# First layer over all pieces, then the second layer in blocks of 512 tokens with a seven-product second matmul, on one pool of 4 KB tiles

## The chip, the cores and the metric

The kernel runs on one core of one Trainium2 chip. The metric is the device time of one execution in microseconds (us); the time of the kernel before is the median of its runs. All on-chip work is written in Bass and Tile: the program's text gives each engine's work, a scheduler at build time sets the order in each engine's queue, and a queue is then executed in that order.

## What is computed

A chunked state-space scan (a small recurrent attention) feeds two feed-forward layers. With 4 sequences of 768 tokens there are 3072 tokens of 256 features.

```python
attn_out = _attn_ref(x, a, B, C)               # scan over chunks of 32 tokens, 8 heads of 32
x = attn_out.transpose(0, 2, 1, 3).reshape(3072, 256)
h = x @ w_in1                                  # 256 -> 2048
x = np.maximum(0.01 * h, h) @ w_out1           # 2048 -> 256
h = np.maximum(x @ w_in2, 0.0)                 # 256 -> 2048
out = (h * h) @ w_out2                         # 2048 -> 256
```

The reference computes in double precision where weights are double. The kernel reaches its accuracy by splitting each operand into a high and a low part (both fp32r), so that each product of two operands is three matmuls: high x low, high x high and low x high.

## The kernel before

**Pieces and scans.** The tokens are cut into 12 pieces of 256 tokens (`NP`, `TP`). `scan_piece` computes the scan of one piece in 20 or 22 steps (`QN`; it is a generator, and each `yield` ends a step). Its chain is: scaled copies (`him`, `ch`, L324 and L325, on ScalarE), the low part `kmx` (L331, VectorE), four small DMAs that lay it out block-diagonally (`diag`, L318, issued by SyncE), 32 matmuls `S` (L348, L349), the masked products `mk` (L358, VectorE), `mkh` (L360, ScalarE) and `mkl` (L365, VectorE), 48 matmuls `Y` (L373 to L375), the state (`d1s` L377 on ScalarE, a scan `stt` L213 on VectorE, `shl` L382 and L384, a transpose L386), four more small DMAs of the state (`sbd`, L318), 32 matmuls into `Y` (L393, L394, here called `Z`), and at last `yh` (L397, ScalarE) and `yl` (L398, VectorE), which are the first layer's input. A piece's state goes into the next piece. For each later sequence, `sequence_scales` loads its pieces once more (`all`, L276) and takes sums of squares (`sq`, L235).

**Layers.** `Phase` is one layer over a block of one or two pieces (`BLOCKS`: four of one piece, 256 tokens wide, then four of two, 512 wide). Per step, `hmm` makes the first product for one or two tiles `m` of 128 of the 2048 features (L425 to L427, 6 matmuls for each m), `act` evicts it (layer 1: two activations L435 and L436 and a subtraction L441; layer 2: a ReLU L438, a square L439 on VectorE, a copy L440 and the subtraction L441), and `omm` adds the second product for it into the two PSUM tiles `o` (L453, L454, L458, also 6 matmuls for each m), two or three steps later (`LAG`). `finish` writes layer 1's result back over its input (L466, L467) or stores layer 2's (L471, L472).

**Order.** A table gives the order of the blocks; the first digit is the layer, the second the block:

```python
ORDER = "10 11 12 20 13 21 14 22 23 15 24 16 25 17 26 27"
```

Between the steps of this loop the main program advances the scans (`step_to(due(...))`), so that a block's scan is written ahead of its first layer, spread over the time since the block before.

**Weights.** The four matrices come as doubles, in 8 chunks each of 512 KB. `w_step` moves the pipeline on by one chunk: load (L121), two passes on ScalarE (L130, L133), two on VectorE (L141, L142), then high part (L153, ScalarE) and low part (L154, VectorE). All four matrices are needed by the time of the first layer-2 block.

**Memory.** Weights, inputs and working tiles lie in pools of their own (`cp`, `sp`, `wp`, `yp`); the accumulators `o` have one buffer each (pool `po`), the first product three (`ph`), the scan's `S` and `Y` one each (`pz`).

## Time and profile before

| what | value |
| --- | --- |
| median of 3 runs | 634.33 us (633.23 to 635.82) |
| profiled execution, its own time | 637.78 us |
| its span, first to last instruction | 636.1 us |
| TensorE busy | 586.2 us (92%), 4434 matmuls |
| VectorE busy | 402.6 us (63%) |
| ScalarE busy | 372.9 us (59%) |
| DMA queue | 45.76 MB, 27.8% of 16 engines |

A busy TensorE is not TensorE at its peak: a matmul's record runs on while the next one has begun, so that the distance between two starts tells what one costs, not its length. Shares are averages over stages: in the first 100 us ScalarE and VectorE are busy almost all the time, later TensorE is. The difference between the span and the profiled execution's own time (1.7 us) lies outside the program's instructions.

### The profile page before, as it was taken

How to read it: one execution, taken by the hardware profiler on the slowest of the kernel's cores; microseconds unless marked ns; L12 is line 12 of the kernel's file. 1: busy time of each engine (PE TensorE's matmuls, PEld its weight loads, DVE VectorE, ACT ScalarE, POOL GpSimd, SP SyncE). 2: the span in 40 equal slices, each digit the busy share in tenths (PEclk: the TensorE clock that was granted, in tenths of full speed). 3: DMA queues.
4: the chain of work that ended last, by engine and by line, in shares of the span. 5: the costliest groups of instructions: out<-in, count | busy, mean ns of one | idle time of the engine just before them, and what ended most of it. 6: DMA issues, size and time to landing. Idle time of an engine off the chain costs nothing.

```text
span 636.1 us, 11298 instructions
## 1 busy us (share of the span) xinstructions
PE 586.2 (92%) x4434; PEld 516.9 (81%) x4434; DVE 402.6 (63%) x687; ACT 372.9 (59%) x678; POOL 5.2 (1%) x14
## 2 busy tenths in 40 slices
PE   0297698999989999999999999999999999999997
PEld 0287698989989888899988888888888888888885
DVE  6999999995558664576564576564565322555553
ACT  6999998876555545545545555455544433544442
POOL 3000000000000000000000000000000000000000
PEclk9999898999989999999999999999999999999999
DMA  7886565555351412202212212212000000000000
GB/s 272 275 291 195 139 205 98 174 124 127 105 94 40 74 51 26 50 35 42 51 51 26 49 36 25 51 67 26 9 1 9 34 1 1 0 2 0 34 1 33
DMA packets 111396, 46.47 MB, mean 73 GB/s; under 512 B 94320, under 2 KB 101104, under 8 KB 111344
## 3 DMA queue, kind: packets, MB, share of 16 engines
q1 hardware_dynamic: 111344, 45.76, 27.8%
q8 instruction: 35, 0.57, 0.4%
q14 instruction: 17, 0.14, 0.1%
HBM read 36.83 MB, written 3.15 MB: 63 GB/s over the span
## 4 chain that ended last, share of the span: by engine, by line
PE 76%; ACT 9%; DVE 6%; DMA 6%; issue 2%; SPq 1%; DVEq 0%; ACTq 0%
PE o L453 12%; PE hp L425 12%; PE hp L427 12%; PE hp L426 12%; PE o L458 12%; PE o L454 12%; DMA all<-in 2%; DMA in<-in 2%; ACT wst L130 1%; ACT wst L133 1%; ACT sq L235 1%; SPq L318 1%; ACT t L436 1%; ACT gh L435 1%; DVE e L195 1%
## 5 line engine op out<-in xcount | busy, mean ns | idle before, releaser
L441 DVE TENSOR_TENSOR gl<-t,gh 128x512 fp32r<-128x512 f32 x192 | 132.3, 689 | 139.5 <-ACT t L436 85.9
L435 ACT ACTIVATE gh<-hp 128x512 fp32r<-128x512 f32 x96 | 57.2, 596 | 84.1 <-PE o L454 75.6
L425 PE MATMUL hp<-yl,wh1i 128*128 128x256 f32 (+1 forms) x256 | 89.5, 350 | 10.8 <-DVE yl L398 4.6
L440 ACT CAST gh<-t 128x512 fp32r<-128x512 f32 x96 | 59.5, 620 | 66.3 <-DVE t L439 56.2
L439 DVE TENSOR_TENSOR t<-t 128x512 f32<-128x512 f32 x96 | 66.2, 689 | 43.4 <-ACT t L438 43.1
L438 ACT ACTIVATE t<-hp 128x512 f32<-128x512 f32 x96 | 57.4, 598 | 56.7 <-PE hp L427 54.5
L453 PE MATMUL o<-gh,wl1o 128*128 128x256 f32 (+1 forms) x256 | 84.9, 347 | 4.5 <-DVE wl1o L154 3.6
L426 PE MATMUL hp<-yh,wh1i 128*128 128x256 f32 (+1 forms) x256 | 88.6, 346 | 0.0
L427 PE MATMUL hp<-yh,wl1i 128*128 128x256 f32 (+1 forms) x256 | 88.4, 345 | 0.0
L426 PE MATMUL hp<-yh,wh2i 128*128 128x256 f32 (+1 forms) x256 | 86.0, 336 | 0.0
L425 PE MATMUL hp<-yl,wh2i 128*128 128x256 f32 (+1 forms) x256 | 86.0, 336 | 0.0
L427 PE MATMUL hp<-yh,wl2i 128*128 128x256 f32 (+1 forms) x256 | 86.0, 336 | 0.0
L453 PE MATMUL o<-gh,w2o 128*128 128x256 f32 (+1 forms) x256 | 83.6, 343 | 1.6 <-DVE yl L467 1.5
L454 PE MATMUL o<-gh,wh1o 128*128 128x256 f32 (+1 forms) x256 | 83.0, 340 | 0.0
L454 PE MATMUL o<-gh,w2o 128*128 128x256 f32 (+1 forms) x256 | 81.9, 336 | 0.0
L425 PEld LDWEIGHTS hp<-yl,wh1i 128*128 128x128 f32 x256 | 51.3, 200 | 16.7 <-DVE ss L256 3.8
L458 PE MATMUL o<-gl,wh1o 128*128 128x256 f32 (+1 forms) x256 | 60.5, 339 | 0.0
L458 PE MATMUL o<-gl,w2o 128*128 128x256 f32 (+1 forms) x256 | 60.3, 336 | 0.0
L453 PEld LDWEIGHTS o<-gh,wl1o 128*128 128x128 f32 x256 | 48.9, 191 | 10.6 <-DVE wl1o L154 4.7
L436 ACT ACTIVATE t<-hp 128x512 f32<-128x512 f32 x96 | 57.1, 594 | 0.0
L426 PEld LDWEIGHTS hp<-yh,wh1i 128*128 128x128 f32 x256 | 51.3, 200 | 5.1 <-issue 0.3
L427 PEld LDWEIGHTS hp<-yh,wl1i 128*128 128x128 f32 x256 | 51.0, 199 | 5.1
(123 smaller groups left out, 984.8 us busy)
## 6 DMA issues: line engine op xcount, KB each, us to landing
in<-in SPq DMA_DIRECT2D x12, 640.0 KB, 4.6
in<-in SPq DMA_DIRECT2D x12, 512.0 KB, 3.4
all<-in SPq DMA_DIRECT2D x15, 384.0 KB, 3.7
wst<-w1i SPq DMA_DIRECT2D x8, 512.0 KB, 7.9
wst<-w1o SPq DMA_DIRECT2D x8, 512.0 KB, 5.8
wst<-w2o SPq DMA_DIRECT2D x8, 512.0 KB, 5.1
wst<-w2i SPq DMA_DIRECT2D x8, 512.0 KB, 4.7
out_t<-ob SPq DMA_DIRECT2D x8, 256.0 KB, 2.2
```

The costliest lines, as they stand in the source:

```text
L425: nc.tensor.matmul(hp, wh, self.xl[:, :, k], start=(k == 0), stop=False)
L426: nc.tensor.matmul(hp, wh, self.xh[:, :, k], start=False, stop=False)
L427: nc.tensor.matmul(hp, wl, self.xh[:, :, k], start=False, stop=(k == KI - 1))
L435: nc.scalar.activation(gh, hp, AF.Lrelu)
L436: nc.scalar.activation(t, hp, AF.Lrelu)
L438: nc.scalar.activation(t, hp, AF.Relu)
L439: nc.vector.tensor_tensor(t, t, t, ALU.mult)
L440: nc.scalar.copy(gh, t)
L441: nc.vector.tensor_tensor(gl, t, gh.bitcast(F32), ALU.subtract)
L453: nc.tensor.matmul(self.o[d], wl, gh, start=(m == 0), stop=False)
L454: nc.tensor.matmul(self.o[d], wh, gh, start=False, stop=False)
L458: nc.tensor.matmul(self.o[d], wh, gl, start=False, stop=(m == KO - 1))
```

## The change

All of layer 1 comes first, block after block (`BLOCKS` is now six blocks of one piece and three of two), with the scans `RATE` = 1.5 steps per tile `m` ahead; then all of layer 2, in six groups of 512 tokens. Layer 2's second product is written by Strassen's algorithm: features `j` and `j + 8`, the two halves of the outputs and the two halves of the tokens make a 2 x 2 by 2 x 2 block product, which takes seven block products (of 128 x 128 by 256 tokens) where the plain form has eight. For that, the weights of `w_out2` get four sums (`split_w1`), the squared activations get four sums `ts` (`act` of `Two`), and the seven results are added up at the end of a group (`finish` of `Two`). The square goes from VectorE to ScalarE. The result of layer 1 is kept in fp32 (`yf`) and split by `split_y` for a whole group. Weights, piece inputs and working tiles come from one pool, `heap`, of 46 tiles of 4 KB per partition. Weights of layer 2 are prepared in smaller portions (`w_one`) while layer 1 runs.

```diff
@@ -34,12 +34,17 @@
 E23 = float(1 << 23)
 QN = [22] * NPC + [20] * (NP - NPC)
 
-BLOCKS = [1, 1, 1, 1, 2, 2, 2, 2]
-GROUPS = [[0, 1], [2, 3], [4], [5], [6], [7]]
-
-ORDER = "10 11 12 20 13 21 14 22 23 15 24 16 25 17 26 27"
+BLOCKS = [1, 1, 1, 1, 1, 1, 2, 2, 2]
+NG = NP // 2
 LAG = {1: 2, 2: 3}
+LAG2 = 2
 W_AHEAD = 4
+RATE = 24 / KO
+NHEAP = 46
+
+
+A11, A12, A22, S1, S3, S2, S4 = 1, 3, 2, 4, 5, 6, 7
+T1, T3, T2, T4 = range(4)
...
-    wp = ctx.enter_context(tc.tile_pool(name="wp", bufs=8))
-    yp = ctx.enter_context(tc.tile_pool(name="yp", bufs=2))
+    heap = ctx.enter_context(tc.tile_pool(name="heap", bufs=NHEAP))
...
+
+    def big(shape, dtype, name):
+        return heap.tile(shape, dtype, tag="b", name=name)
...
     def split_w1():
 
-        nm, c, sl, w0, w1 = w_half.pop(0)
+        nm, c, w0, w1 = w_half.pop(0)
         nc.vector.scalar_tensor_tensor(w0, w1, 3, w0, ALU.logical_shift_left, ALU.bitwise_or)
-        nc.vector.scalar_tensor_tensor(w0, w1, -(1 << 31), w0, ALU.bitwise_and, ALU.bitwise_or)
-        w_full.append((nm, c, sl, w0.bitcast(F32)))
+        if nm != "2o":
+            nc.vector.scalar_tensor_tensor(w0, w1, -(1 << 31), w0, ALU.bitwise_and, ALU.bitwise_or)
+            w_full.append((nm, c, w0.bitcast(F32)))
+            return
+        a = big([P, 8, P], F32, "wa")
+        nc.vector.scalar_tensor_tensor(
+            a[:, 0:4].rearrange("p (k d) f -> p k (d f)", k=2).bitcast(I32),
+            w1, -(1 << 31), w0, ALU.bitwise_and, ALU.bitwise_or,
+        )
+        nc.vector.scalar_tensor_tensor(a[:, S1], a[:, 0], -1.0, a[:, A22], ALU.mult, ALU.subtract)
+        nc.vector.tensor_tensor(a[:, S3], a[:, A11], a[:, 0], ALU.subtract)
+        nc.vector.scalar_tensor_tensor(a[:, S2], a[:, S1], -1.0, a[:, A11], ALU.mult, ALU.subtract)
+        nc.vector.tensor_tensor(a[:, S4], a[:, A12], a[:, S2], ALU.subtract)
+        w_full.append((nm, c, a[:, 1:8]))
 
     def split_w2():
 
-        nm, c, sl, w = w_full.pop(0)
+        nm, c, w = w_full.pop(0)
         if nm == "2o":
-            t = w_last[c] = wp.tile([P, 2, 2, 256], F32R, tag="w", name="w2o")
+            h, l = w_done[nm, c] = tuple(big([P, 7, P], F32R, x) for x in ("wh", "wl"))
+        else:
+            t = w_done[nm, c] = big([P, 2, 2, 256], F32R, f"w{nm}")
             h, l = t[:, 0], t[:, 1]
-        else:
-            h, l = w_hi[nm][sl], w_lo[nm][sl]
         nc.scalar.activation(h, w, AF.Copy)
         nc.vector.tensor_tensor(l, w, h.bitcast(F32), ALU.subtract)
...
+    def w_one():
+
+        if w_full:
+            split_w2()
+        elif w_half:
+            split_w1()
+        elif w_loaded:
+            split_w()
+        if wq and not w_loaded:
+            load_w()
...
-        w = sp.tile([P, U * 2 * T], F32, tag="in2", name="in2")
+        w = big([P, U * 2 * T], F32, "in2")
...
         def finish(self):
-            n = self.n
-            if self.layer == 1:
-                xh, xl = self.xh, self.xl
-                for d in range(2):
-                    o = self.o[d].rearrange("p (a t) -> p a t", t=TP)
-                    nc.scalar.copy(xh[:, :, d], o)
-                    nc.vector.tensor_tensor(xl[:, :, d], o, xh[:, :, d].bitcast(F32), ALU.subtract)
-                return xh, xl
+            g = self.p0 // 2
+            if g not in yf:
+                yf[g] = big([P, 2, KI, TP], F32, "yf")
+            to = yf[g][:, self.p0 % 2 : self.p0 % 2 + self.n]
             for d in range(2):
-                ob = ap_.tile([P, 512], F32, tag="t", name="ob", bufs=3)[:, :n]
-                (nc.scalar.copy if d == 0 else nc.vector.tensor_copy)(ob, self.o[d])
-                nc.sync.dma_start(out[d * P : (d + 1) * P, self.t0 : self.t0 + n], ob)
...
+    def split_y(g):
+        y = yf.pop(g)
+        h, l = (big([P, 2, KI, TP], F32R, t) for t in ("xh", "xl"))
+        nc.scalar.copy(h, y)
+        nc.vector.tensor_tensor(l, y, h.bitcast(F32), ALU.subtract)
+        ys[g] = h, l
+
+    class Two:
+
+
+        def __init__(self, g):
+            self.t0 = g * 2 * TP
+            self.x = ys.pop(g)
+            self.g = {}
+            self.m = None
+
+        def hmm(self, j):
+            self.h = []
+            for m in (j, j + KO // 2):
+                hp = ph.tile([P, 512], F32, tag="h", name="hp")
+                in_products(hp, "2i", m, *self.x)
+                self.h.append(hp)
+
+        def act(self, j):
+            b = ap_.tile([P, 4, TP], F32, tag="t", name="b")
+            for i, hp in enumerate(self.h):
+                nc.scalar.activation(b[:, 2 * i : 2 * i + 2], hp.rearrange("p (n t) -> p n t", n=2), AF.Relu)
+            nc.scalar.activation(b, b, AF.Square)
+            bh, bl = (big([P, 3, TP], F32R, x) for x in ("bh", "bl"))
+            th, tl = (big([P, 4, TP], F32R, x) for x in ("th", "tl"))
+            t = big([P, 4, TP], F32, "ts")
+            nc.scalar.copy(bh, b[:, 1:])
+            nc.vector.tensor_tensor(t[:, 0:2], b[:, 1:3], b[:, 0:1].to_broadcast([P, 2, TP]), ALU.subtract)
+            nc.vector.tensor_tensor(t[:, T2], b[:, 2], t[:, T1], ALU.add)
+            nc.vector.tensor_tensor(t[:, T4], b[:, 3], t[:, T2], ALU.subtract)
+            nc.scalar.copy(th, t)
+            nc.vector.tensor_tensor(bl, b[:, 1:], bh.bitcast(F32), ALU.subtract)
+            nc.vector.tensor_tensor(tl, t, th.bitcast(F32), ALU.subtract)
+            self.g[j] = (bh, bl), (th, tl)
+
+        def omm(self, j):
+            if self.m is None:
+                o = [po.tile([P, 512], F32, tag=f"o{d}", name=f"o{d}") for d in range(2)]
+                y = pz.tile([P, 4, TP], F32, tag="Y", name="Ym")
+                self.m = [t.rearrange("p (n t) -> p n t", n=2) for t in o] + [y]
+            o26, o13, o754 = self.m
+            b, t = self.g.pop(j)
+            wh, wl = w_done["2o", j]
+            first, last = j == 0, j == KO // 2 - 1
+            for o, s, (h, l), i, new in (
+                (o13[:, 0], A11, b, 0, True),
+                (o13[:, 1], S4, b, 1, False),
+                (o26[:, 0], A12, b, 2, True),
+                (o26[:, 1], S2, t, T2, False),
+                (o754[:, 0], S3, t, T3, True),
+                (o754[:, 1], S1, t, T1, False),
+                (o754[:, 2], A22, t, T4, True),
+            ):
+                s -= 1
+                nc.tensor.matmul(o, wl[:, s], h[:, i], start=first and new, stop=False, skip_group_check=True)
+                nc.tensor.matmul(o, wh[:, s], h[:, i], start=False, stop=False, skip_group_check=True)
+                nc.tensor.matmul(o, wh[:, s], l[:, i], start=False, stop=last, skip_group_check=True)
+
+        def finish(self):
+            o26, o13, o754 = self.m
+            r = sp.tile([P, 5, TP], F32, tag="in1", name="r")
+            two = [P, 2, TP]
+
+            def store(i, d, n):
+                nc.sync.dma_start(out[d * P : d * P + P, self.t0 + n * TP : self.t0 + n * TP + TP], r[:, i])
+
+            nc.scalar.copy(r[:, 2], o13[:, 0])
+            nc.vector.tensor_tensor(r[:, 0:2], r[:, 2:3].to_broadcast(two), o26, ALU.add)
+            store(0, 1, 1)
+            nc.vector.tensor_tensor(r[:, 2:4], r[:, 1:2].to_broadcast(two), o754[:, 0:2], ALU.add)
+            nc.vector.tensor_tensor(r[:, 3], r[:, 3], o13[:, 1], ALU.add)
+            store(3, 1, 0)
+            nc.vector.tensor_tensor(r[:, 1:5:3], r[:, 2:3].to_broadcast(two), o754[:, 1:3], ALU.add)
+            store(1, 0, 0)
+            store(4, 0, 1)
+
...
-
-    pos, starts = 0, []
-    for layer, i in order:
-        if layer == 1:
-            starts.append((pos, sum(QN[: blocks[i][0] + blocks[i][1]])))
-        pos += KO * blocks[i][1]
+    starts = [(KO * p0, sum(QN[: p0 + n])) for p0, n in blocks]
 
     def due(at):
-        for (a, na), (b, nb_) in zip(starts, starts[1:]):
-            if at < b:
-                return na + -(-(nb_ - na) * (at - a) // (b - a))
-        return sum(QN)
+        return max([nb - int(RATE * (b - at)) if b > at else nb for b, nb in starts] + [0])
 
...
+    def need(nm, m):
+        while (nm, m) not in w_done:
+            (w_step if nm[0] == "1" else w_one)()
...
-    for layer, i in order:
-        p0, n = blocks[i]
-        yh, yl = ys.pop(i) if layer == 2 else ys[i]
-        ph_ = Phase(layer, p0, n, yh, yl)
+    for i, (p0, n) in enumerate(blocks):
+        ph_ = One(p0, n)
         for m in range(0, KO, 2 // n):
             ms = list(range(m, m + 2 // n))
-            while (ph_.wo, m // 2) in wq or any((ph_.wo, m // 2) == v[:2] for v in w_loaded + w_half + w_full):
-                w_step()
+            need("1i", m // 2)
             ph_.hmm(ms)
             pos += 2
             ph_.act(ms)
             step_to(due(pos + 2))
-            pend.append((ph_, ms))
+            pend.append((ph_, ms, ms[-1] == KO - 1))
+            if len(pend) > LAG[n]:
+                need("1o", pend[0][1][-1] // 2)
             second(LAG[n])
-            acc += 1.0 if len(wq) > 18 else 0.4
+            first_w = wq[:1] and wq[0][0][0] == "1" or any(v[0][0] == "1" for v in w_loaded + w_half + w_full)
+            acc += 1.0 if first_w else (0.3 if i < len(blocks) - 1 else 1.5)
             while acc >= 1:
                 acc -= 1
-                w_step()
+                (w_step if first_w else w_one)()
+            if i == len(blocks) - 1 and m == KO - 4:
+                split_y(0)
+        if p0 % 2 + n == 2:
+            ys.pop(p0 // 2)
+    second(0)
+
+    for g in range(NG):
+        ph_ = Two(g)
+        for j in range(KO // 2):
+            need("2i", j // 2)
+            need("2i", (j + KO // 2) // 2)
+            ph_.hmm(j)
+            pend.append((ph_, j, j == KO // 2 - 1))
+            if len(pend) > LAG2:
+                need("2o", pend[0][1])
+            second(LAG2)
+            ph_.act(j)
+            w_one()
+            if j == 5 and g + 1 < NG:
+                split_y(g + 1)
     second(0)
```

The class `One` is layer 1 of `Phase` with the same matmuls; `in_products` has the six matmuls of `hmm`.

The change moves instructions. **The start, on SyncE's DMA queue.** The program before begins with these rows (`in` are the two inputs of a piece, `wst` a chunk of weights, `all` the second load of a sequence's pieces):

```order
L176 DMA in_116<-in 128x1280
L177 DMA in_117<-in 128x1024
L121 DMA wst<-w1i 128x2x256 x6
L176 DMA in_290<-in 128x1280
L121 DMA wst<-w1i 128x2x256 x2
L177 DMA in_291<-in 128x1024
L121 DMA wst<-w1o 128x512 x3
```

The changed program begins with:

```order
L196 DMA in_107<-in 128x1280
L295 DMA all<-in 128x3x256
L197 DMA in_108<-in 128x1024
L118 DMA wst<-w1i 128x2x256 x4
L197 DMA in_281<-in 128x1024
L196 DMA in_280<-in 128x1280
L337 DMA xbh<-xh 32x16x32 x2
L118 DMA wst<-w1i 128x2x256 x4
```

A load for the second sequence now stands ahead of the first piece's second input, and the last four chunks of the first matrix stand behind the second piece's first input and behind two of its small DMAs (`xbh`), where before six of eight chunks came at once.

**One piece's scan, on ScalarE.** Before, for the fifth piece, with its state steps `d1s` and `shl`:

```order
L436 ACTIVATE t<-hp 128x512
L377 ACTIVATE d1s<-Y 128x32x8
L235 ACTIVATE sq,mx<-all 128x768
L382 CAST shl<-stt 128x16x16
L207 ACTIVATE d1s<-stt 128x32
```

In the changed program, for the fifth piece:

```order
L461 ACTIVATE t<-hp 128x512
L344 ACTIVATE ch<-in_2415,sc 128x512
L254 ACTIVATE sq,mx<-all 128x768
L396 ACTIVATE d1s<-Y 128x32x8
L401 CAST shl<-stt 128x16x16
```

The squares of a later sequence, which wait for the load `all`, stood between the two steps and now stand ahead of both; so it is for the pieces four to eight.

**Layer 2, on ScalarE and on VectorE.** In the changed program ScalarE's rows of one step and the next are:

```order
L518 ACTIVATE b<-hp 128x512 x2
L519 ACTIVATE b<-b 128x1024
L523 CAST bh<-b 128x768
L527 CAST th<-ts 128x1024
L518 ACTIVATE b<-hp 128x512
L495 CAST xh<-yf 128x1024
```

and VectorE's, where a group ends (`r` is the group's result):

```order
L524 TENSOR_TENSOR ts<-b 128x512
L564 TENSOR_TENSOR r<-r,o_5199 128x512
L525 TENSOR_TENSOR ts<-b,ts 128x256
L566 TENSOR_TENSOR r<-r,Ym 128x512
L526 TENSOR_TENSOR ts<-b,ts 128x256
L567 TENSOR_TENSOR r<-r,o_5200 128x256
L569 TENSOR_TENSOR r<-r,Ym 128x2x256
L528 TENSOR_TENSOR bl<-b,bh 128x768
```

Before, a step of layer 2 was a ReLU and a copy of 512 columns on ScalarE and a square and a subtraction on VectorE; now `th` waits for VectorE's sums `ts`, and the additions of a group's end stand between these sums.

## Rows read from the trace of the kernel before

**Rows 1.** Windows: stretch, length, busy us of PE, PEld, DVE, ACT, POOL; PEclk is the granted clock.
```profile
31.60:104.90 73.30, 60.77 (x617) 57.72 (x617) 71.55 (x149) 70.73 (x140) 0.00 (x0) 0.98 0.69 198
104.90:250.00 145.10, 138.67 (x1324) 131.82 (x1325) 100.88 (x169) 90.05 (x169) 0.00 (x0) 0.98 0.40 91
250.00:631.90 381.90, 381.88 (x2382) 322.99 (x2380) 203.41 (x311) 185.51 (x324) 0.00 (x0) 1.00 0.12 25
```

**Rows 2.** Timeline of PE: first layer-1 matmul of the first and of the third piece.
```profile
31.65 0.58 PE L425 MATMUL hp<-yl,wh1i 128*128 128x256 f32 x1 [2.45 <-DVE yl L398]
...
104.89 0.51 PE L425 MATMUL hp<-yl,wh1i 128*128 128x256 f32 x1 [2.16 <-DVE yl L398]
```

**Rows 3.** Timeline of PE: two matmuls of 512 columns, the twelfth apart.
```profile
521.37 0.39 PE L425 MATMUL hp<-yl,wh1i 128*128 128x512 f32 x1
...
524.09 0.39 PE L425 MATMUL hp<-yl,wh1i 128*128 128x512 f32 x1
```

**Rows 4.** Timeline of PE: two matmuls of 256 columns, the eleventh apart, each with its own weights.
```profile
300.93 0.28 PE L425 MATMUL hp<-yl,wh2i 128*128 128x256 f32 x1
...
302.25 0.28 PE L427 MATMUL hp<-yh,wl2i 128*128 128x256 f32 x1
```

**Rows 5.** Groups by line: one weight load on PE (busy us, mean ns).
```profile
L454 PEld LDWEIGHTS o<-gh,w2o 128*128 128x128 f32 x256 | 48.5, 190 | 4.8
```

**Rows 6.** Groups by line: one weight pass on ScalarE and one on VectorE.
```profile
L130 ACT ACTIVATE wst<-wst 128x512 f32<-128x512 f32 x32 | 22.0, 688 | 1.1 <-DMA wst<-w2o 1.1
L141 DVE SCALAR_TENSOR_TENSOR wst<-wst 128x512 int32<-128x512 int32 x32 | 21.4, 684 | 0.0
```

**Rows 7.** Waits of PE from 104.9 us to the end: total us, times, longest.
```profile
PE Y L393 <- DMA sbd<-t: 4.0, 2, 2.9
...
PE o L453 <- DVE yl L467: 1.5, 1, 1.5
PE o L453 <- ACT ob L471: 0.9, 1, 0.9
```

**Rows 8.** Timelines of PE and ACT: the fifth piece, last Y matmul to first Z matmul.
```profile
167.92 0.18 PE L375 MATMUL Y<-mkh,xbl 128*128 128x48 f16 x1
...
172.54 0.84 ACT L235 ACTIVATE sq<-all 128x768 bf16<-128x768 f32 x1 [4.01 <-DMA all<-in]
...
179.75 0.18 PE L393 MATMUL Y<-qh,sbd 128*128 128x32 f16 x1 [2.93 <-DMA sbd<-t]
```

**Rows 9.** Timelines of PE, SP and DVE: the eleventh piece, last Y matmul to the landed state.
```profile
425.77 0.18 PE L375 MATMUL Y<-mkh,xbl 128*128 128x48 f16 x1
...
429.38 2.62 SPq L318 DMA_DIRECT2D sbd<-t  x4
...
433.54 0.75 DVE L341 SCALAR_TENSOR_TENSOR xl<-in,sc,xh 128x512 f16<-128x512 f32 x1 [1.55 <-DMA sbd<-t]
```

**Rows 10.** Groups by line and form: durations of evictions by width (busy us, mean ns).
```profile
L438 ACT ACTIVATE t<-hp 128x512 f32<-128x512 f32 x96 | 57.4, 598 | 56.7 <-PE hp L427 54.5 <-DVE gl L441 1.4 <-ACT yh L466 0.3
L440 ACT CAST gh<-t 128x512 fp32r<-128x512 f32 x96 | 59.5, 620 | 66.3 <-DVE t L439 56.2 <-PE o L458 6.5 <-PE o L454 2.7
L360 ACT CAST mkh<-in 128x768 f16<-128x768 f32 x12 | 10.0, 831 | 2.1 <-DVE in L358 2.0
L439 DVE TENSOR_TENSOR t<-t 128x512 f32<-128x512 f32 x96 | 66.2, 689 | 43.4 <-ACT t L438 43.1
L467 DVE TENSOR_TENSOR yl<-o,yh 128x256 fp32r<-128x256 f32 x8 | 3.1, 412 | 0.0
```

**Rows 11.** Timeline of DVE and ACT: a square and the copy that waits for it.
```profile
469.49 0.69 DVE L439 TENSOR_TENSOR t<-t 128x512 f32<-128x512 f32 x1 [0.60 <-ACT t L438]
470.27 0.62 ACT L440 CAST gh<-t 128x512 fp32r<-128x512 f32 x1 [0.82 <-DVE t L439]
```

**Rows 12.** Timeline: the end, last matmuls and last copy.
```profile
631.32 0.61 PE L458 MATMUL o<-gl,w2o 128*128 128x512 f32 x2
...
631.97 0.69 DVE L471 COPY ob<-o 128x512 f32<-128x512 f32 x1 [2.62 <-PE o L458]
```

More of the change, by code (lines that the diff above doesn't have):

```diff
@@ L491, in piece_y @@
     def piece_y(p):
-        i = block_of[p]
-        return lambda: tuple(t[:, p - blocks[i][0]] for t in y_of(i))
-    order = [(int(v[0]), int(v[1:])) for v in ORDER.split()]
+        return lambda: tuple(t[:, p % 2] for t in y_of(p))
     loaded = {0: load_piece(0)}
```

141 lines of the change are left out of this document (61 added, 80 removed).

## Prediction

> **What bounds the kernel now.** I read the windows first. From the first matmul of layer 1 at 31.65 us to that of the third piece at 104.89 us [rows 2], VectorE is busy 71.55 and ScalarE 70.73 of 73.30 us, and TensorE only 60.77 [rows 1]: here the two evicting engines, loaded with weight preparation, set the pace. After that TensorE is busy nearly all the time, and the others half of it or less [rows 1]. So the start is priced by ScalarE's and VectorE's instructions, and the rest by distances between matmul starts.
>
> Those distances come from the timeline. Twelve matmuls of 512 columns take 524.09 - 521.37 = 2.72 us, 0.2267 each [rows 3]; eleven of 256 columns, every one with weights of its own, take 1.32 us, 0.120 each [rows 4]. The record of one is longer than its distance, so busy time is not used for this.
>
> From 104.89 to the last matmul's end at 631.9 [rows 12] are 527.0 us. In them stand 1536 matmuls of 512 columns (348.2 us) and 1152 of 256 (138.2), together 486.4. The other 40.6 us are three things: listed waits, 4.0 + 1.5 + 0.9 = 6.4 [rows 7]; lost clock, since the mean granted clock was 0.98 of 2.4 GHz over 145.1 us [rows 1], worth 2.9; and 31.3 for the scans' small matmuls and small gaps, which I leave as they are, because the change keeps those matmuls.
>
> **The change part by part.**
>
> *Matmuls.* The plain second product of a layer-2 pair of features is 12 matmuls for each half of 256 tokens; by seven products it is 21 of 256 columns for both halves. The program goes from 1536 to 1152 matmuls of 512 and from 1536 to 2160 of 256: -384 x 0.2267 + 624 x 0.120 = -12.2 us. In the changed order 21 more of them lie behind the third piece's first matmul (1797 of 256 against 1152), so of this -87.0 + 77.4 = **-9.6** falls into the part that TensorE bounds; the rest is in the stretch that it doesn't bound, and is worth nothing there.
>
> The Trainium skill speaks against this step: "TensorE: Matmul & The Clock Gate", section "Back-to-back issue gap", gives for a stream of weight loads and matmuls about 81 ns at 128 columns and 131 ns at 512. On the line between them 256 columns would be an estimated 98 ns, and the program's change -384 x 131 + 624 x 98 ns = +10.9 us. The trace does not agree: 226.7 and 120 ns in just such a stream; the measurement decides.
>
> *First stretch.* Weight preparation is spread out, so fewer passes stand ahead of the third piece: on ScalarE 15 weight passes at 0.688 [rows 6] and four evictions at about 0.60 [rows 10] fewer, -12.7; on VectorE eight passes at 0.684 [rows 6] fewer, -5.5. Against that, six instructions of the second piece (three squares, `ch`, `xh`, `him`) now stand ahead of the first `yh`. By the rows of 512 columns, 0.60 to 0.69 each [rows 6, 10], they start layer 1 up to 4.1 later, and the load `all` and the later chunks of the first matrix push the same way on SyncE's queue. Both engines are full here, so the one that is relieved less decides: VectorE, -5.5 + 4.1 = **-1.4**. Ends: -8.6 (ScalarE's relief counts in full) and +4.1 (no relief counts).
>
> *Scans.* Behind each last `Y` matmul a chain runs over ScalarE, VectorE and four DMAs before `Z` can start, and TensorE needs other matmuls meanwhile. Undisturbed the chain took 433.54 - 425.77 = 7.8 us, 2.62 of it in the state's DMAs [rows 9]; in the fifth piece 179.75 - 167.92 = 11.8, because ScalarE stood 4.01 us in front of a square that waits for `all`, and TensorE stood still 2.93 us [rows 8]. In the changed order the matmuls between the last `Y` and the first `Z` of pieces four to twelve amount to 7.6, 7.7, 8.2, 9.4, 8.1, 9.55, 7.7, 9.55 and 7.5 us. At 7.8 the chain would cost 0.7 us in all, at 11.8 it would cost 9 x 11.8 - 75.3 = 30.9. The squares now stand ahead of both state steps, which takes away what was seen in [rows 8]; they can still be late there, and `Y` then is late with them. I take 8.9, nearer the undisturbed row: 1.3 + 1.2 + 0.7 + 0.8 + 1.2 + 1.4 = 6.6 us.
>
> *Layer 2.* A step `j` holds TensorE 12 x 0.2267 + 21 x 0.120 = 5.24 us. ScalarE: two ReLUs at 0.60; the square and the copy `th`, of 1024 columns, at an estimated 1.04 each, by the slope from 0.620 (512) to 0.831 (768); `bh`, of 768, at 0.83 [rows 10]. Beside `bh` run VectorE's sums `ts`, 0.69 + 0.41 + 0.41 [rows 10], with a hop of 470.27 - 470.18 = 0.09 [rows 11] on either side. The chain is 1.20 + 1.04 + 0.09 + 1.51 + 0.09 + 1.04 = 4.97, so 0.27 us per step are to spare, and the step costs nothing while that holds. The square on ScalarE has no other cover; without it each 0.1 us over costs 48 x 0.1 = 4.8 us. At a group's end VectorE and ScalarE read the banks in turn, 0.41 + 0.69 + 0.69 + 0.41 [rows 10] with hops and two sums `ts` between them some 3.3 us, against the 2.72 us of one `hmm` before the next group writes: 0.6 x 5 = 3.0. The first step of the layer costs about 1.0, and the last about 1.5: chain and `tl` (4.97 + 1.2) behind the last `hmm`, against two second products (5.0) ahead. Together 5.5; ends 1.5 (only the last step shows) and 12 (each step is some 0.14 over as well).
>
> The sums of `w_out2`'s weights fall into the last block of layer 1: VectorE 8 x (2 x 0.68 + 4 x 0.27 + 1.1) = 28.3, by the rows for 512 and 256 columns [rows 6, 10], and 16 x 0.69 for evictions, 39.3 of the 16 x 12 x 0.2267 = 43.5 us of matmuls there: covered, by 4 us.
>
> *Waits and clock behind the third piece.* Listed waits go from 6.4 to 6.6 + 5.5 = 12.1 (the old ones belong to the old order). Of the 2.9 us of clock I take half back, since the two long stops that precede it go while shorter ones come: -1.5. Together **+4.2**.
>
> *End.* Before, one copy of 0.69 us lay between the last matmul and the stores [rows 12]; now it is 0.41 + 0.69 + 0.69 + 0.41 + 0.69 = 2.89: **+2.2**.
>
> *Sum:* -1.4 - 9.6 + 4.2 + 2.2 = **-4.6 us** against a span of 636.1, hence 631.5, and 633.2 with the 1.7 around it. The profiled run (637.78) was 3.45 above the median of 634.33; the difference on that median gives **629.7 us**.
>
> **The rivals.**
>
> 1. *The scans' chain becomes the wait that replaces the one removed* (slower). With all of layer 1 first, no layer-2 block lies between two pieces, and the order leaves 7.5 to 9.55 us of cover. If the chain takes 10.5, two thirds of the way from [rows 9] to [rows 8], the waits are 19.2 instead of 6.6: +12.6, 642 us; at 11.8 it is 654. It makes the kernel slower than before by over 0.5% from a mean chain of about 10 us. For it speaks that the pieces crowd, with weights on the same engines; against it, that less weight work is left per microsecond. Chance 0.24.
> 2. *ScalarE bounds layer 2.* If the step takes 5.5 us, 0.26 x 48 = +12.5, 642 us. For it: only 0.27 us to spare, and waits for tiles of the shared pool stand in the same queues. Against: one ReLU of the next step can run while `th` waits for `ts`. Chance 0.10.
> 3. *The order works better than I price it.* The early relief counts to the end of -8.6 (7.2 more), and the scans cost 0.7 (5.9 less): 629.7 - 13.1, about 616 us. For it: the chain of 7.8 was seen. Chance 0.21.
> 4. *The narrow matmuls wait for their weight loads.* A load's record is 190 ns [rows 5]; if that were the distance, 1008 matmuls x 0.070 = +71 us, 700 us. Against it: [rows 4], eleven in a row at 120 ns. Chance 0.02, any milder form of it included. The rule of the Trainium skill that is given above ("TensorE: Matmul & The Clock Gate") is such a milder form: +10.9 for -12.2 would be an estimated 653 us, and [rows 3, 4] speak against it too.
>
> **How the numbers follow.** My forecast has 0.43, with its own range from 622 to 637: the first stretch alone moves it between -7.2 and +5.5, and layer 2 between -4.0 and +6.5. The range over all is 614 to 645: it takes in rival 3 and rivals 1 and 2 at their prices, and leaves out scans at 11.8 and rival 4. A measurement of this kernel can tell about 0.5% from no change, 3.2 us: below 631.2 is faster, above 637.5 slower. Of the forecast's 0.43 about 0.27 is faster, 0.14 the same and 0.02 slower; rival 3 adds 0.21 to faster; rivals 1, 2 and 4 give 0.29 to slower, 0.05 to the same and 0.02 to faster, where the chain comes out only a little longer. So faster 0.50, same 0.19, slower 0.31.
>
> **What the changed profile would show.** The matmul step is right if the distances in layer 2 stay at 0.227 and 0.120 and a step `j` begins every 5.24 us; rival 2 is right if TensorE waits there for `tl` or `bl` in most steps. The scans' term is right if TensorE's waits for `sbd` come to some 6 us in all, rival 1 if to 15 or more. The first stretch is right if the third piece's first matmul stands near 103.5 us, rival 3 if near 97. From the last matmul's end to the end of the span should be 6.4 us, against 4.2. The forecast is wrong if waits appear that I put at nothing: TensorE waiting for prepared weights, or a copy held by the pool of 46 tiles.

## The result, and the profile after

| | kernel before | changed kernel |
| --- | --- | --- |
| median | 635.13 us (633.16 to 637.13, 10 runs) | 639.90 us (638.06 to 641.32, 10 runs) |
| ratio to before | | 1.0070 (95% interval 1.0049 to 1.0092) |
| profiled span | 636.1 us | 638.9 us |
| third piece's first matmul of layer 1 | 104.89 us | 116.68 us |
| from there to the last matmul's end | 527.0 us | 517.4 us |
| last matmul's end to the end of the span | 4.2 us | 4.9 us |

The forecast was 629.7 us, faster. The kernel is slower, by 0.7%. The last three rows of the table are three of the stretches in which the prediction counted: +11.8, -9.7 and +0.7 us make the +2.8 of the spans. So the steps behind the third piece paid more than was forecast, and the first stretch lost more than all of it. The medians lie further apart than the spans, 4.8 us: the profiled execution of the kernel before, at 637.78 us, stood 2.7 above its median, that of the changed kernel, at 640.69, only 0.8. Some 2 us of the loss therefore stand in no pair of rows below.

The windows of the changed kernel (stretch, length, busy us of PE, PEld, DVE, ACT, POOL, then the granted clock, the DMA share and GB/s):

```profile
31.60:75.00 43.40, 29.82 (x253) 28.11 (x250) 36.67 (x60) 34.29 (x65) 0.00 (x0) 0.76 0.69 210
75.00:105.00 30.00, 24.55 (x260) 23.71 (x260) 23.34 (x48) 24.32 (x50) 0.00 (x0) 0.89 0.70 189
...
381.00:633.90 252.90, 252.87 (x1586) 229.05 (x1584) 191.55 (x268) 197.91 (x253) 0.00 (x0) 1.00 0.03 11
```

and the same two first windows of the kernel before:

```profile
31.60:75.00 43.40, 33.39 (x318) 31.00 (x319) 42.97 (x95) 43.38 (x89) 0.00 (x0) 0.99 0.72 218
75.00:105.00 30.00, 27.48 (x301) 26.82 (x301) 28.68 (x56) 27.44 (x52) 0.00 (x0) 0.96 0.63 168
```

Before, ScalarE and VectorE were full from 31.6 to 75 us. Now ScalarE is busy 34.29 of 43.40 us and VectorE 36.67, and still TensorE does less (253 matmuls against 318). None of the three is full: they wait for one another. What they wait for begins on SyncE. Its queue from the start (start, us, engine, line, operation):

```profile
0.73 0.40 SPq L196 DMA_DIRECT2D in<-in  x1
1.19 0.42 SPq L295 DMA_DIRECT2D all<-in  x1
1.65 0.49 SPq L197 DMA_DIRECT2D in<-in  x1
2.18 3.08 SPq L118 DMA_DIRECT2D wst<-w1i  x4
5.30 0.88 SPq L197 DMA_DIRECT2D in<-in  x1
20.58 0.33 SPq L196 DMA_DIRECT2D in<-in  x1
32.42 1.38 SPq L337 DMA_DIRECT2D xbh<-xh  x2
33.85 2.58 SPq L118 DMA_DIRECT2D wst<-w1i  x4
```

Between 6 and 32 us the queue issues one load. Chunks 5 to 8 of the first matrix are asked for at 33.85 us. The kernel before had asked for all eight by 17.4:

```profile
1.64 4.46 SPq L121 DMA_DIRECT2D wst<-w1i  x6
...
16.22 1.20 SPq L121 DMA_DIRECT2D wst<-w1i  x2
```

ScalarE of the changed kernel, from the first `yh` to the first eviction of layer 1:

```profile
33.16 0.67 ACT L416 ACTIVATE yh<-Y,fac 128x512 fp32r<-128x512 f32 x1
33.73 1.21 ACT L162 ACTIVATE w1i<-wst 128x512 fp32r<-128x512 f32 x2
38.36 0.69 ACT L127 ACTIVATE wst<-wst 128x512 f32<-128x512 f32 x1 [3.43 <-DMA wst<-w1i]
...
46.55 0.61 ACT L460 ACTIVATE g<-hp 128x512 fp32r<-128x512 f32 x1
```

It stands 3.43 us for a late chunk, and 16 weight passes lie in its queue ahead of the eviction at 46.55 us. Not one high part (`w1i`, L162) was made before `yh`. In the kernel before 20 passes were done ahead of `yh`, eight stood between it and the first eviction, and that came at 34.94:

```profile
29.82 0.67 ACT L397 ACTIVATE yh<-Y,fac 128x512 fp32r<-128x512 f32 x1
...
34.94 0.58 ACT L435 ACTIVATE gh<-hp 128x512 fp32r<-128x512 f32 x1
```

TensorE of the changed kernel shows the same from its side: the first matmul of layer 1, the one that waits for that eviction, and the third piece's first.

```profile
34.84 0.55 PE L437 MATMUL hp<-yl,w1i 128*128 128x256 f32 x1 [2.69 <-DVE yl L417]
...
47.70 0.58 PE L437 MATMUL hp<-yl,w1i 128*128 128x256 f32 x1 [5.26 <-ACT t L461]
...
116.68 0.35 PE L437 MATMUL hp<-yl,w1i 128*128 128x256 f32 x1
```

The first matmul comes 3.2 us later than in [rows 2], the first eviction 11.6 us later, the third piece 11.8 us later. From first eviction to third piece it is 70 us in both kernels, so the loss stands before the first eviction and is then carried along. That these two stretches are equal is partly chance: up to the third piece the changed kernel's ScalarE makes 61 weight passes, that of the kernel before 78. In the variants of the changed kernel below, the stretch takes 66 to 75 us.

TensorE's waits from 116.7 us to the end, which answer to [rows 7] (total us, times, longest):

```profile
PE Y L412 <- DMA sbd<-t: 3.4, 6, 0.9
PE S L309 <- DVE in L377: 0.9, 1, 0.9
PE Y L392 <- ACT mkh L379: 0.6, 1, 0.6
PE o L475 <- ACT yf L490: 0.3, 1, 0.3
```

They sum to 5.2 us, and none is in layer 2. There TensorE is busy 252.87 of 252.90 us.

### The profile page after: what moved, and what is told of

Its sections match the earlier page's. It is cut to its first block, busy times and chain, and to the rows that moved or that the text cites. A ratio compares the mean times of both kernels' runs of the same rounds, so it can differ in the third digit from the quotient of the medians.

```text
span 638.9 us, 11725 instructions
## 1 busy us (share of the span) xinstructions
PE 581.0 (91%) x4674; PEld 525.7 (82%) x4674; DVE 469.1 (73%) x782; ACT 452.4 (71%) x723; POOL 5.2 (1%) x14
## 4 chain that ended last, share of the span: by engine, by line
PE 71%; DVE 8%; ACT 7%; DMA 7%; SPq 4%; issue 2%; DVEq 0%; ACTq 0%
PE hp L437 11%; PE hp L438 11%; PE hp L439 11%; PE o L475 5%; PE o L481 5%; PE o L476 5%; PE o L553 4%; PE o L552 4%; SPq L337 4%; PE o L551 4%; PE Ym L553 3%; PE Ym L552 3%; PE Ym L551 3%; DMA sbd<-t 3%; DMA in<-in 1%
## 5 line engine op out<-in xcount | busy, mean ns | idle before, releaser
L437 PE MATMUL hp<-yl,w1i 128*128 128x256 f32 (+1 forms) x288 | 95.7, 332 | 12.6 <-ACT t L461 9.4
L462 DVE TENSOR_TENSOR g<-t,g 128x512 fp32r<-128x512 f32 x96 | 65.6, 685 | 42.5 <-ACT t L461 41.9
L475 PE MATMUL o<-g,w1o 128*128 128x256 f32 (+1 forms) x288 | 90.0, 332 | 6.5 <-DVE w1o L163 2.6
L439 PE MATMUL hp<-yh,w1i 128*128 128x256 f32 (+1 forms) x288 | 95.0, 330 | 0.3 <-DVE w1i L163 0.3
L438 PE MATMUL hp<-yh,w1i 128*128 128x256 f32 (+1 forms) x288 | 94.6, 329 | 0.0
L476 PE MATMUL o<-g,w1o 128*128 128x256 f32 (+1 forms) x288 | 88.6, 327 | 0.0
L437 PE MATMUL hp<-xl,w2i 128*128 128x512 f32 x192 | 75.3, 392 | 0.0
L438 PE MATMUL hp<-xh,w2i 128*128 128x512 f32 x192 | 75.2, 392 | 0.0
L439 PE MATMUL hp<-xh,w2i 128*128 128x512 f32 x192 | 74.7, 389 | 0.0
L437 PEld LDWEIGHTS hp<-yl,w1i 128*128 128x128 f32 x288 | 57.6, 200 | 19.1 <-ACT t L461 10.1
L529 DVE TENSOR_TENSOR tl<-ts,th 128x1024 fp32r<-128x1024 f32 x48 | 58.8, 1226 | 12.6 <-ACT th L527 12.6
L475 PEld LDWEIGHTS o<-g,w1o 128*128 128x128 f32 x288 | 56.6, 197 | 10.9 <-DVE w1o L163 2.7
L481 PE MATMUL o<-g,w1o 128*128 128x256 f32 (+1 forms) x288 | 63.6, 328 | 0.0
L439 PEld LDWEIGHTS hp<-yh,w1i 128*128 128x128 f32 x288 | 57.5, 200 | 4.3 <-DVE w1i L163 0.5
L438 PEld LDWEIGHTS hp<-yh,w1i 128*128 128x128 f32 x288 | 57.6, 200 | 3.6
L476 PEld LDWEIGHTS o<-g,w1o 128*128 128x128 f32 x288 | 56.8, 197 | 3.6
```

The lines of the kernel that those rows point to most:

```text
L437: nc.tensor.matmul(hp, wh[:, k, c], xl[:, :, k], start=(k == 0), stop=False)
L438: nc.tensor.matmul(hp, wh[:, k, c], xh[:, :, k], start=False, stop=False)
L439: nc.tensor.matmul(hp, wl[:, k, c], xh[:, :, k], start=False, stop=(k == KI - 1))
L462: nc.vector.tensor_tensor(g[:, 1], t, g[:, 0].bitcast(F32), ALU.subtract)
L475: nc.tensor.matmul(self.o[d], wl[:, c], gh, start=(m == 0), stop=False)
L476: nc.tensor.matmul(self.o[d], wh[:, c], gh, start=False, stop=False)
```

## The experiments

**Theory A: the shared pool couples what has nothing to do with one another.** The pool gives out its tiles in the order in which the program's text asks for them. A tile that the text asks for after `yh` and `yl` of the first piece can't be written before these two have their places, and they get them when the first `yh` is about to be written, at 33 us. The text asks for chunk 5, and for every high part, after `yh`. The scheduler, which otherwise pulls loads and passes ahead, can't pull these. The rule itself stands in no trace; what can be tested is what would follow from it. **Rival B: it is the work itself**, the second piece's preparation ahead of the first `yh` and two full engines. **Rival C: the seven products cost waits in layer 2** that eat their gain.

The kernel before ran beside all of them; its medians in these comparisons lie between 635.1 and 637.4 us, so the ratios are compared rather than the times.

| kernel | first `yh` | passes after it, before the first eviction | first eviction | third piece | time | ratio to before |
| --- | --- | --- | --- | --- | --- | --- |
| before | 29.82 | 8 | 34.94 | 104.9 | 635.1 | 1 |
| changed | 33.16 | 16 | 46.55 | 116.7 | 639.9 | 1.0070 (1.0049 to 1.0092) |
| e1, own pool for y | 34.16 | 5 | 38.72 | 107.7 | 629.2 | 0.9879 (0.9838 to 0.9920) |
| e2, eight loads first | 40.53 | 16 | 54.55 | 121.3 | 644.3 | 1.0115 (1.0075 to 1.0155) |
| e3, plain second product | 33.41 | 16 | 46.80 | 114.4 | 646.1 | 1.0146 (1.0101 to 1.0191) |
| e4, own pool and eight loads | 39.98 | 2 | 44.76 | 113.4 | 634.7 | 0.9956 (0.9933 to 0.9979) |
| e5, own pool for `w1i` | 33.95 | 13 | 48.46 | 118.2 | 640.5 | 1.0067 (1.0042 to 1.0092) |
| e7, own pool for y, fixed tiles apart | 32.16 | 4 | 36.88 | 106.5 | 626.1 | 0.9819 (0.9782 to 0.9857) |
| e8, fixed tiles apart only | 30.22 | 16 | 44.54 | 110.8 | 636.2 | 0.9990 (0.9967 to 1.0012) |

All places are in us of the profiled run, read from ScalarE's and TensorE's timelines; the times are medians. e10 and e11 start from e7, e9 from the kernel before; they stand further below.

**e1: a pool of their own for `yh` and `yl`.**

```diff
-            ys[p // 2] = tuple(big([P, 2, KI, TP], F32R, t) for t in ("yh", "yl"))
+            ys[p // 2] = tuple(yp.tile([P, 2, KI, TP], F32R, tag=t, name=t) for t in ("yh", "yl"))
...
-NHEAP = 46
+NHEAP = 42
...
+    yp = ctx.enter_context(tc.tile_pool(name="yp", bufs=2))
```

> Edit: yh and yl, the first layer's inputs, get a pool of their own (4 tiles, the shared pool has 42 instead of 46); nothing else. Theory A (the shared pool hands its tiles out in the program's order, so that the last four chunks of the first matrix, and every high part of its weights, had to wait for the first yh, 33.2 us): the loads of chunks 5 to 8 stand behind the second piece's input (about 20 us) and no longer behind xbh (32.4 us), and the high parts are spread ahead of yh; the waits of TensorE for the eviction t (9.4 us) and for prepared weights go; the third piece's first matmul comes at 105 to 108 instead of 116.7 us, the time falls by 8 to 11 to 629 to 632 us. Rival B (it is the work itself, the second piece's preparation ahead of the first yh and two full engines): that work stays, the third piece stays after 114 us, the time within 2.5 us of 639.9.

Measured: 629.24 us, ratio 0.9879; third piece at 107.73. SyncE's queue (line numbers are one higher than in the changed kernel):

```profile
20.54 0.33 SPq L197 DMA_DIRECT2D in<-in  x1
20.92 2.51 SPq L119 DMA_DIRECT2D wst<-w1i  x4
```

and ScalarE from the last pass ahead of `yh` to the first eviction:

```profile
33.59 0.67 ACT L163 ACTIVATE w1i<-wst 128x512 fp32r<-128x512 f32 x1
34.16 0.67 ACT L417 ACTIVATE yh<-Y,fac 128x512 fp32r<-128x512 f32 x1
...
38.72 0.60 ACT L461 ACTIVATE g<-hp 128x512 fp32r<-128x512 f32 x1 [0.41 <-PE hp L440]
```

The late chunks now follow the second piece's input, at 20.92 us, instead of `xbh`, at 33.85; 19 passes are done before `yh` instead of 8, and the eviction waits for TensorE, no longer for passes. The first matmul did not come sooner (35.76 against 34.84 us). The same work, with the tiles handed out from two pools, is 1.9% faster, which is more than the change had lost. This is what theory A expected, and rival B is out as the main cause: 9.0 of the 11.8 us at the third piece go without any work being taken away. The other 2.8 stay. From the third piece's first matmul to the last matmul's start it is 514.4 us here and 517.1 in the changed kernel, with 19 matmuls of 256 columns fewer behind that point (2.3 us): behind the third piece little else changed.

**e2, e4, e5: which half?** e2 asks for all eight chunks first; e4 does that with the pool of e1; e5 frees the high parts alone.

```diff
-W_AHEAD = 4
+W_AHEAD = 8
```

> Edit: W_AHEAD 8 instead of 4, so that all eight chunks of the first matrix are asked for before the first yh; the pool stays shared. The loads now stand at the head of the queue, the high parts still behind yh. Theory A with its two halves: the loads' half goes (ScalarE's idle 3.4 us behind yh, and the passes on late chunks that stand ahead of the first eviction), the high parts' half stays: third piece at 108 to 113 us, time 632 to 636 us. Rival B: within 2.5 us of 639.9. If the loads alone were the cause, it equals the kernel with a pool of its own for y.

> Edit: both, own pool for yh and yl and W_AHEAD 8. Theory A: the third piece's first matmul at 103 to 106 us, time 627 to 631 us, at least 1 us under the own pool alone. Rival B: not under 637.

Both missed: 644.25 and 634.73 us, by theory A's numbers and by rival B's. With eight chunks there early, their passes went ahead of the first piece's `mkh` on ScalarE, and TensorE waited for that. This is its longest wait in e2 (total us, times, longest):

```profile
PE Y L392 <- ACT mkh L379: 12.2, 1, 12.2
```

and the same wait in the first 125 us of the changed kernel:

```profile
PE Y L392 <- ACT mkh L379: 4.8, 1, 4.8
```

The first matmul moved from 34.84 to 42.21 us. Early loads are no good by themselves; what is in place early is also worked on early. Nor does e2 take the late loads away, as it was meant to: the chunks that now stand behind `xbh` are those of the next matrix, `w1o`, and ScalarE waits for them in the same place.

```profile
46.73 0.68 ACT L127 ACTIVATE wst<-wst 128x512 f32<-128x512 f32 x1 [4.43 <-DMA wst<-w1o]
```

Of the 16 passes ahead of e2's first eviction six are high parts and ten belong to these chunks. e4 shows much the same delay beside the gain of the own pool: its first matmul is 6.0 us later than e1's (e2: 7.4 later than the changed kernel's), and its first eviction comes 4.8 us after `yh`, against 4.6 in e1. My expectation had the sign of the loads' half wrong.

```diff
-            t = w_done[nm, c] = big([P, 2, 2, 256], F32R, f"w{nm}")
+            t = w_done[nm, c] = (wp.tile([P, 2, 2, 256], F32R, tag="w", name="w1i") if nm == "1i" else big([P, 2, 2, 256], F32R, f"w{nm}"))
...
-NHEAP = 46
+NHEAP = 38
...
+    wp = ctx.enter_context(tc.tile_pool(name="wp", bufs=8))
```

> Edit: only the high and low parts of the first matrix get a pool of their own (8 tiles, the shared pool has 38); yh, yl and the loaded chunks stay in the shared pool, so that chunks 5 to 8 are still loaded behind xbh. It parts the two halves of theory A. If the high parts behind yh are what costs (8 passes of ScalarE and the low parts after 33 us, in front of the first evictions): third piece at 108 to 112 us, 631 to 635 us. If the late loads are what costs: third piece still at 114 to 117, 637 to 640 us. The smaller shared pool may cost something in layer 2, which the distance from the third piece's first matmul to the end shows (517 us in the changed kernel).

Measured: 640.45 us, the third piece at 118.2: the second of the two cases, a little above its range. With the high parts free and the chunks late there are still 13 passes and an idle stretch ahead of the eviction, as ScalarE's timeline of e5 shows:

```profile
40.08 0.68 ACT L128 ACTIVATE wst<-wst 128x512 f32<-128x512 f32 x1 [4.61 <-DMA wst<-w1i]
...
48.46 0.58 ACT L461 ACTIVATE g<-hp 128x512 fp32r<-128x512 f32 x1
```

So freeing one half leaves the block of passes in front of the eviction (late chunks of the first matrix in e5, late high parts and late chunks of the next matrix in e2), and only a pool of their own for `yh` and `yl`, which frees both, takes it away: 5 passes are left in e1, 2 in e4, 4 in e7. From the third piece's first matmul to the last matmul's start e5 takes 517.5 us and the changed kernel 517.1: the smaller pool costs nothing there.

**e8 and e7: the four fixed tiles.** `xbh`, `xbl`, `kbd` and `sbd` live through the whole program and were asked for first, so in theory A the first piece's second input had to wait behind them, and `all` slipped ahead of it. They go back to the pool `cp` (38 tiles are left in the shared pool in e7, 42 in e8).

```diff
-    xbh = big([P, U, 4, T], F16, "xbh")
+    xbh = cp.tile([P, U, 4, T], F16, name="xbh")
...
```

> Edit: only the four fixed tiles leave the shared pool; yh, yl and the weights share it. The load all moves behind the first chunks, the late chunks and the high parts stay late. Theory A: 1 to 3 us under the changed kernel, 637 to 639 us (third piece 114 to 116). If the load all were the main cause: 632 or less.

> Edit: own pool for yh and yl as before, and the four tiles that live for the whole program (xbh, xbl, kbd, sbd) out of the shared pool too. These four are asked for first and written by memsets, so in theory A the first piece's second input had to wait for them, and the load all went ahead of it; him started at 14.1 us instead of 11.2. Now all stands behind the first four chunks. Expected: him at 11 to 12 us, the first matmul of layer 1 at 33 to 34 instead of 35.8, the third piece at 105 to 106, 2 us under the kernel with the pool for y alone: 626 to 628 us against 629. Rival: the transfer of all is hidden, 629.

e8 gives 636.2 us, by the ratios 0.8% under the changed kernel; the first matmul is at 31.90 us instead of 34.84, the third piece at 110.8 instead of 116.7. That is about twice what I expected. Only 2.0 of these 5.9 us are there at the first eviction, where 16 passes still stand; the rest comes behind it, and why is not shown. With the own pool (e7) it is 626.11 us, ratio 0.9819, as expected: the lowest of this study, though its interval overlaps e1's. e7's queue, from the first piece's second input on:

```profile
1.18 0.42 SPq L198 DMA_DIRECT2D in<-in  x1
1.64 2.62 SPq L119 DMA_DIRECT2D wst<-w1i  x4
4.30 0.66 SPq L296 DMA_DIRECT2D all<-in  x1
```

and `him` on ScalarE:

```profile
11.28 0.72 ACT L344 ACTIVATE him<-in,sbp 128x512 f16<-128x512 f32 x1
```

`him` starts at 11.28 us instead of 14.10. The gains don't add: e8 moves the third piece by 5.9 us, e1 by 9.0, both together by 10.2.

**e3: the plain second product.** Layer 2 with 12 matmuls of 512 columns for a pair of features, without the sums.

```diff
-                nc.tensor.matmul(o, wl[:, s], h[:, i], start=first and new, stop=False, skip_group_check=True)
...
+            for k in range(2):
+                for d in range(2):
+                    nc.tensor.matmul(o, w[:, 1, k, c], h, start=(j == 0 and k == 0), stop=False)
+                    nc.tensor.matmul(o, w[:, 0, k, c], h, start=False, stop=False)
+                    nc.tensor.matmul(o, w[:, 0, k, c], l, start=False, stop=last)
```

> Edit: the changed kernel with layer 2's second product in its plain form, 12 matmuls of 512 columns for each pair of features instead of 21 of 256; no sums of weights or activations, no additions at a group's end. Left out of the change is thus the seven-product form alone. If layer 2 is bound by TensorE at the distances of before, 48 x (12 x 0.2267 - 21 x 0.120) = +9.6 us, less some 2 at the end: 647 to 650 us, the first 120 us as in the changed kernel. If the seven products had cost waits in layer 2 that ate their gain (rival C): 640 or less.

Measured: 646.12 us, 1.0146, just under what I expected; against the changed kernel's 1.0070 the seven products are worth some 0.8% or 5 us of time. The profiled runs show where: from the third piece's first matmul to the last matmul's start 525.8 us against 517.1, so 8.7 of the counted 9.6; the end, behind the last matmul, is 1.0 us shorter in the plain form, and its third piece came 2.3 us sooner. Up to the first eviction the two are alike (46.80 and 46.55 us); where the 2.3 come from behind it was not followed up, so a difference of that size between two orders says little. Rival C is out.

**e9: the same fault put into the kernel before.** Its pool `wp` also holds `yh` and `yl` of the first group and of one later group.

```diff
-    wp = ctx.enter_context(tc.tile_pool(name="wp", bufs=8))
+    wp = ctx.enter_context(tc.tile_pool(name="wp", bufs=10))
...
-        gt[g] = tuple(yp.tile([P, 2, KI, TP], F32R, tag=f"y{g % 3}", name=t) for t in ("yh", "yl"))
+        gt[g] = tuple((wp if g % 3 == 0 else yp).tile([P, 2, KI, TP], F32R, tag="w" if g % 3 == 0 else f"y{g % 3}", name=t) for t in ("yh", "yl"))
```

> Edit of the kernel before, the other way round: its pool wp (chunks as loaded, and w2o) also holds yh and yl of the first two pieces and of one later group, 10 tiles instead of 8 and the pool of that group gone; order of blocks, scans and matmuls stay as before. In the order only four chunks of the first matrix are now loaded ahead of the first yh, the other four behind it. Theory A: late chunks cost here as well, through evictions behind weight passes or matmuls that wait for weights; third piece's first matmul at 110 to 117 us instead of 104.9, time 640 to 647 us. Rival B (the late start belongs to the order with all of layer 1 first): within 3 us of the kernel before.

Measured: 649.26 us, 1.0184 (1.0157 to 1.0212), third piece at 119.2: slower than expected, and with the old order of blocks, so the edit costs there too. The way is another one, though. The four chunks were asked for at 20.98 us, nine us ahead of the first `yh` and not behind it as I had said, and the first eviction is in time (35.05 us). The loss shows between the first and the second piece: in its first 160 us TensorE waits 14.9 us for `sq` and 11.3 for `yl`, against 7.0 and 4.6 in the kernel before. Chunks of the last matrix, whose tiles lie in another pool, had moved ahead in the queue as well. So e9 shows that moving `yh` and `yl` into a pool with the weights costs time, but it does not bear out the rule of theory A as I worded it: on the chip a tile that was asked for later could be written long before `yh`. If the rule holds, it holds for the order that the scheduler writes, and not as a wait on the chip.

**e10 and e11: from e7 on.**

```diff
-W_AHEAD = 4
+W_AHEAD = 2
```

> Edit: the kernel with own pool for yh and yl and fixed tiles apart, and W_AHEAD 2 instead of 4. Eight chunks ahead put passes in front of the first piece's mkh (TensorE waited 12.2 us there instead of 4.8 to 6.3); with two chunks only four passes stand there instead of seven. If passes ahead of mkh set the first matmul, it comes 1 to 2 us sooner (32 to 33 us), and the time is 624 to 626 us; if the third piece is set by the sum of passes until then, nothing changes: 626.

```diff
-RATE = 24 / KO
+RATE = 28 / KO
```

> Edit: the same kernel with RATE 28 / KO instead of 24 / KO, the scans 1.75 steps per tile m ahead: they end earlier before their block needs them. TensorE's listed waits for the scans' state came to 3.4 us in the changed kernel. If more distance hides them, 1 to 3 us less: 623 to 625; if the chain is set by what stands between its steps, the scan of the second piece presses harder on the first stretch: 626 to 629.

e10: 629.18 us, ratio 0.9869 (0.9850 to 0.9888). The first matmul came at 31.59 us, even sooner than said, and the third piece at 109.7, 3.3 later than in e7: passes that are not done before `yh` are done after it. The first half was right, its price wrong. e11: 636.6 us, 0.9984 (0.9964 to 1.0004), worse than either expectation. Its profiled run, 632.82 us at a span of 631.0, was the shortest of its ten, so its rows show less than the median's loss. The waits for the scans' state fell, as its waits behind the third piece show, and others came in their place, 7.9 us in all; earlier, TensorE waited 8.4 us for `w1o` (2.5 in e7).

```profile
PE hp L438 <- DVE yl L418: 3.6, 3, 2.3
...
PE Y L413 <- DMA sbd<-t: 1.4, 2, 1.0
```

In e7 the only two there are `sbd` with 4.4 us and `kbd` with 0.6. Of the 5.8 us by which this span is longer than e7's, 0.9 stand ahead of the third piece and 5.0 between it and the last matmul, and the listed waits explain 2.9 of these. Why more distance for the scans costs time is thus not shown.

## Why the prediction was wrong

**The step that failed** is the first stretch: "Both engines are full here, so the one that is relieved less decides: VectorE". It gave -1.4, with ends of -8.6 and +4.1. Measured: +11.8. The step took the engines' being full in [rows 1] as a property of the stretch, and priced only how many instructions stand ahead. That number was near: ahead of the third piece's first matmul ScalarE makes 61 weight passes instead of 78 (I had taken 15 fewer) and VectorE eight weight instructions fewer, as counted. But the relief bought no time: ScalarE, with less to do, stood still for a late load and then had the passes on the late chunks in front of the first eviction.

Of the 13.2 us between -1.4 and +11.8 the runs part two. The first is the shared pool's order, which the sum did not have. The rows of the order that stand in the section on the change show it: "the last four chunks of the first matrix stand behind the second piece's first input and behind two of its small DMAs". I named that push and gave it no price of its own. Its price could have been bounded: `xbh` waits for the second piece's `xh`, which stands on ScalarE behind the first piece's `sbd` copies, and these ran at 26.85 us in the kernel before, so chunk 5 could hardly be asked for before about 29, and 14 passes at some 0.58 us from start to start stood in the changed kernel between its landing and the first eviction. e1 shows that tiles alone, no work, made the difference: 9.0 us.

The second, some 4.2 us, is the relief itself. In e1, without the pool's order, the first matmul comes 4.1 us later than before, the size that I gave the second piece's preparation (e7 brings back 1.8 of these 4.1 by moving the fixed tiles, so that part of it was the load `all`). From there to the third piece e1 takes 72.0 us and the kernel before 73.2: the relief that I put at 5.5 was worth 1.3. ScalarE is busy 61.8 of these 72.0 us and VectorE 66.1, so neither is full any longer. That they had been full before because the scheduler could fill every gap with weight passes is my reading; no run tests it.

**The other steps:**

- *Matmuls, -9.6*: right. Behind the third piece 1152 matmuls of 512 and 1797 of 256 columns stand, as counted, and the step `j` takes 626.32 - 621.06 = 5.26 us against 5.24. These two rows are the first second-product matmul of two successive steps of the last group:

```profile
621.06 0.28 PE L551 MATMUL o<-bh,wl 128*128 128x256 f32 x1
...
626.32 0.28 PE L551 MATMUL o<-bh,wl 128*128 128x256 f32 x1
```

  The sustained spacing that the Trainium skill gives ("TensorE: Matmul & The Clock Gate", section "Back-to-back issue gap"), by which the prediction estimated that this step would cost time, does not agree with the runs: e3, with the plain product, is slower than the changed kernel by 0.8%.

- *Scans, +6.6*: the chain near, the waits half. From last `Y` to first `Z` the nine pieces took 8.0 to 10.5 us, 9.0 on average, where I took 8.9; the listed waits for `sbd` are 3.4 us, where I took 6.6. Rival 1, which needs a mean of about 10, fell.

- *Layer 2, +5.5*: too high; it cost nothing that the waits list. ScalarE's chain fits, about as worked out: before the second ReLU of a step it waits for TensorE, 0.39 us on average, where I had 0.27 to spare.

```profile
621.26 0.60 ACT L518 ACTIVATE b<-hp 128x512 f32<-128x512 f32 x1 [0.34 <-PE hp L439]
```

  At a group's end the banks close one after the other, so their reading starts before the group's last matmul (428.83 us). The copy on ScalarE:

```profile
428.24 0.35 ACT L563 COPY r<-o 128x256 f32<-128x256 f32 x1
```

  the third addition on VectorE:

```profile
430.84 0.42 DVE L567 TENSOR_TENSOR r<-r,o 128x256 f32<-128x256 f32 x1
```

  and TensorE's first write into the next group:

```profile
431.70 0.28 PE L551 MATMUL o<-bh,wl 128*128 128x256 f32 x1
```

  The copy begins while the group's last matmuls run, and with the third addition the bank `o13` is free at 431.26, 0.4 us before it is written; I had it 0.6 late. Rival 2 fell with it.

- *End, +2.2*: +0.7, for the same reason: the banks are read as they close. The first addition starts at 633.05 us, 0.7 before the last matmul does (633.75).

- *Waits, clock and small gaps behind the third piece*: forecast 12.1 of listed waits and 32.7 of the rest, 44.8 in all; measured 5.2 listed and 40.6 in all, as in the kernel before. So the waits were put 7 us too high and the rest nearly 3 too low, and the term of +4.2 came to nothing. In the experiments this sum, here to the last matmul's start (40.3 in the changed kernel), is 38.9 to 40.9 us, but for e9 (37.2) and e11 (44.3): none of the pools raises it.

Rival 3, the early relief in full, named the right place with the wrong sign. The rival on the slow side was the wrong one: the wait that replaced the one removed was an eviction behind weight passes, not the scans' chain. That 639.9 lies near the 642 us of rivals 1 and 2 is chance, for neither of their waits is there. My list of what could prove the forecast wrong did name it ("a copy held by the pool of 46 tiles"), but as something put at nothing.

## What to carry to other kernels

A shared pool saves memory, but it can also make an order: in this kernel loads and passes whose tiles were asked for later were not pulled ahead of what had asked before, and `yh` and `yl` in a pool of their own brought 1.9%. Keep early, freely movable work (loads and conversions of weights) out of a pool in which it stands behind a tile that is written late, and look in the order of the queues for loads that have moved behind a small DMA that waits. And an engine that is full in a stretch of the old profile is full of work that the scheduler could move there; before taking that as the stretch's price, ask whether the change still lets it, and what would set the pace with less of that work.

## What had not been expected of the hardware

The clock fell, too. TensorE stood still from 42.4 to 47.7 us, up to the late eviction, and the granted clock is 0.50 (the level of 1.2 GHz) from 45.6 to 66.1 us. In the kernel before it is 0.50 only from 74.2 to 77.6 us in this stretch. Between the first matmul of layer 1 and the third piece's first, the matmuls of 256 columns that start 0.17 to 0.23 us after one another, mostly 0.213 where it is 0.120 at the granted clock of 1.00, number 91 in the changed kernel and 62 in the kernel before; over 0.120 they cost 8.5 us against 5.6. In e1 they number 54 and cost 5.0.

What this costs in time is not shown. From the first eviction to the third piece it is 70 us in both kernels, and 69.0 in e1, so the slow matmuls do not show in the third piece's time.

The granted clock has to be read with care at the start of a program. In the kernel before, the matmuls from 32.0 to 36.5 us also start 0.213 apart, and the profile gives 1.00 for that stretch; in the changed kernel it is so up to 38.5 us. The 0.99 and 0.76 of the windows from 31.6 to 75 us are not quite comparable for that reason, and the distances between starts are the surer sign.
